# GpSimd makes the low parts of three operands, and the token mixing's last product uses all 128 rows

## The chip, the cores and the metric

The kernel runs on one core of a Trainium2 chip. The metric is the time on the device in microseconds (us). A core has TensorE (PE; its weight loads, PEld, overlap its matmuls), VectorE (DVE), ScalarE (ACT), GpSimd (POOL) and SyncE (SP), which here issues all DMAs. Each engine works through its own instructions in order and waits on semaphores for the others.

## The reference

Three layers follow one another: an attention with mixed heads, a gated layer (the "first layer" after the attention), and a layer with rotated tokens. The change lies in the gated layer, for 4 images ("batch") of 448 tokens:

```python
h = gelu(x @ w_in)                        # 448 x 768 @ 768 x 1024
u, v = h[..., :512], h[..., 512:]
v_n = (v - mu) / np.sqrt(var + 1e-06) * g_ln
v_s = np.einsum('ts,bsd->btd', w_sg, v_n) + b_sg[None, :, None]   # w_sg: 448 x 448
gated = u * v_s
return x + gated @ w_out                  # 512 x 768
```

The weights w_in, w_out and those of the last layer come as 64-bit floats and are decoded on the chip.

## The kernel before, in words

Every float32 matmul operand is split in two: `cast` (line 531, ScalarE) makes the high part, and `rest` (line 534) subtracts it from the value, which leaves the low part. A product is then three matmuls: high by high, high by low, low by high. `mm` (line 538) issues them into one PSUM tile; all matmuls of the dense layers carry that line.

The work of the dense layers is a list of units (`d.unit`), each a group of matmuls with what follows it: `v_chunk` (128 tokens of v), `u_half` (128 features of u), `gate` (the token mixing for 128 features: products with w_sg, then on VectorE `gt` = ps * g_ln + b_sg, times u) and `out` (128 features of the output, with the residual added). For image b the order is: v chunks, half of the out units of image b - 1, four u units, the other out units, four gates. For image 0 it is v, u, gates; for the last image three out units of image 2 stand behind its gates. Hooks before and after a unit (`d.pre`, `d.post`) hold the rest: loads of x, `split_x` (x of the next image, two blocks of 128 rows after each of three units from the end of u on), `split_wsg` (in the first two u units of image 0), normalisation and split of v, `gate_split` (g, one unit after its gate), stores, and the `tick`s of the decoder. All order is written out by hand: each engine's queue follows the program's order.

The decoder takes blocks of 128 x 256 words through ScalarE (two conversions and the high part) and VectorE (lines 574, 576, 581, 589, 595, 598: two shifts and masks, a mask, a product, a subtraction, an addition). In this part of the kernel all VectorE steps of a decoded block run on VectorE; the blocks of w_out are needed by the first `out` unit, those of the last layer's weights only later.

448 tokens are three blocks of 128 and a last one of 64. The last 64 tokens of two neighbouring images share a block: image b even takes rows 0 to 63 (`p.start` 0), b odd rows 64 to 127. In `norm_split` the tile `vnm` of each holds the high part in its own 64 rows and the low part in the other 64, and w_sg's last 64 rows stand twice in `wsg[3]`. So `(m, wh)` on 128 rows gives high by high and low by high at once, and `(m[p], wl[p])` on 64 rows gives high by low.

Buffers that matter here: x (one per block and part, reused for the next image), g (one per block and part), `gt` (two), the staging tiles of the loads (four; w_sg and x of the next image go through them).

Of the kernel before, what the change touches and what calls it, by code (L numbers as in the profile page):

```python
# [6 lines left out]
F32 = mybir.dt.float32  # L7
F32R = mybir.dt.float32r
# [4 lines left out]
ALU = mybir.AluOpType  # L13
# [3 lines left out]
B, H, S, D = 4, 12, 448, 64  # L17
# [457 lines left out]
class Dense:  # L475
# [71 lines left out]
    def decode(self, src, n, dst, tiles=None):  # L547

        nc, box = self.nc, {}

        def block(pool, i):
            if tiles:
                return tiles(i)
            if i == 0:
                box["hl"] = pool.tile([128, 2, 256], F32R, tag="dh", name="dh", bufs=self.out_bufs)
            return box["hl"][:, i, :n]

        def load(pool):  # L560
            raw = pool.tile([128, 256, 2], U32, tag="draw", name="draw", bufs=self.raw_bufs)
            nc.sync.dma_start(out=raw.rearrange("p n w -> p (n w)")[:, :2 * n], in_=src.bitcast(U32))
            box["raw"] = raw

        def words(pool, part=None):
            raw = box["raw"]
            if part != 1:
                for t in ("a", "low", "p"):
                    box[t] = pool.tile([128, 256], F32, tag="d" + t[0], name="d" + t[0], bufs=self.mid_bufs)[:, :n]
                nc.scalar.activation(out=box["p"], in_=raw[:, :n, 1].bitcast(F32), func=AF.Copy, scale=2.0 ** -112)  # L570
                nc.scalar.activation(out=box["low"], in_=raw[:, :n, 0], func=AF.Copy, scale=2.0 ** -52)
            if part != 0:
                au, pu = (box[t].bitcast(U32) for t in "ap")
                nc.vector.tensor_scalar(out=au, in0=pu, scalar1=3, scalar2=0x7FFFFFF8,
                                        op0=ALU.logical_shift_left, op1=ALU.bitwise_and)
                nc.vector.scalar_tensor_tensor(out=au, in0=pu, scalar=0x80000000, in1=au,  # L576
                                               op0=ALU.bitwise_and, op1=ALU.bitwise_or)

        def value(pool):
            a, p = box["a"], box["p"]  # L580
            nc.vector.tensor_scalar(out=p.bitcast(U32), in0=a.bitcast(U32), scalar1=0xFF800000, scalar2=None,
                                    op0=ALU.bitwise_and)

        def high(pool, part=None):
            if part != 1:
                box["h"] = block(pool, 0)
                nc.scalar.activation(out=box["h"], in_=box["a"], func=AF.Copy)
            if part != 0:
                nc.vector.tensor_tensor(out=box["p"], in0=box["p"], in1=box["low"], op=ALU.mult)

        def low(pool, part=None):
            a, p, h = (box[k] for k in ("a", "p", "h"))
            if part != 1:
                box["lo"] = block(pool, 1)
                nc.vector.tensor_tensor(out=a, in0=a, in1=h.bitcast(F32), op=ALU.subtract)
            if part != 0:
                eng = nc.vector if self.mid_bufs > 1 else nc.gpsimd
                eng.tensor_tensor(out=box["lo"], in0=a, in1=p, op=ALU.add)

        def store(pool):  # L600
            if tiles:
                return
            nc.sync.dma_start(out=dst, in_=box["hl"][:, :, :n].bitcast(F32))

        return load, words, value, high, low, store

    def decode_tiles(self, src, rows, c0, c1, tiles):
# [28 lines left out]
def moe1(d, left, right):  # L636

    tc, nc, io = d.tc, d.nc, d.io
    win_es, tail_es, tail_ps = ExitStack(), ExitStack(), ExitStack()
    win, wsg, wout, xt, uT, vraw, mv, vn, mixed, gt, res = ({} for _ in range(11))  # L640
# [62 lines left out]

    def split_wsg(c):
        raw = res.pop(("wsg", c))
        wsg[c] = [d.pools["w"].tile([128, S], F32R, tag=f"wsg{c}{i}", name="wsg") for i in range(2)]
        d.cast(wsg[c][0], raw)
        d.rest(nc.vector, wsg[c][1], raw, wsg[c][0])

    def load_x(b, k):  # L710
        raw = d.stage(512, "xraw")
# [6 lines left out]
    def split_x(b, k):  # L718
        if k == 0:
            xt[b] = ([], [])  # L720
        raw = res.pop(("x", b, k))
        n = 512 if b % 2 == 0 else S
        h, l = (d.pools["x"].tile([128, 512], F32R, tag=f"x{i}{k}", name="x") for i in range(2))
        d.cast(h[:, :n], raw[:, :n])
        d.rest(nc.vector, l[:, :n], raw[:, :n], h[:, :n])
        xt[b][0].append(h)
        xt[b][1].append(l)

# [62 lines left out]
    def gate(b, f):  # L791
        if f == 0:
            gt[b] = ([], [])
        m, p = mixed[b]
        fs = slice(128 * f, 128 * f + 128)
        ps = d.ps()
        terms = []
        for c in range(3):
            (h, l), (wh, wl) = vn[b, c], wsg[c]
            terms += [(h[:, fs], wh), (h[:, fs], wl), (l[:, fs], wh)]  # L800
        wh, wl = wsg[3]
        terms += [(m[:, fs], wh), (m[p, fs], wl[p])]
        d.mm(ps[:, :S], terms)
        t = d.pools["t"].tile([128, S], F32, tag="gt", name="gt")
        nc.vector.scalar_tensor_tensor(out=t, in0=ps[:, :S], scalar=small["gln"][:, f:f + 1], in1=small["bsg"],
                                       op0=ALU.mult, op1=ALU.add)
        nc.vector.tensor_tensor(out=t, in0=t, in1=uT[b][f], op=ALU.mult)
        res["g", b, f] = t

    def gate_split(b, f):  # L810
        t = res.pop(("g", b, f))
        h, l = (d.pools["g"].tile([128, S], F32R, tag=f"g{f}{i}", name="g") for i in range(2))
        d.cast(h, t)
        d.rest(nc.vector, l, t, h)
        gt[b][0].append(h)
        gt[b][1].append(l)

# [22 lines left out]
    for b in range(B + 1):  # L840
        if b < B:
            nv = 4 if b % 2 == 0 else 3
            v0[b] = len(d.units)
            for c in range(nv):
                d.post(U(v_chunk, b, c), v_stats, b, c)
        if b:
            o0[b - 1] = [U(out, b - 1, m) for m in range(KD // 2 if b != B - 1 else NO2)]
        if b < B:
            u0[b] = len(d.units)
            for f in range(KF):  # L850
                U(u_half, b, f)
        if 0 < b < B - 1 or b == B:
            o0[b - 1] += [U(out, b - 1, m) for m in range(KD // 2, KD)]
        if b < B:
            g0[b] = len(d.units)
            for f in range(KF):
                i = U(gate, b, f)
                late.append((d.post, i + 1, gate_split, b, f))
        if b == B - 1:
            o0[b - 1] += [U(out, b - 1, m) for m in range(NO2, KD)]  # L860
# [3 lines left out]
    for c in range(4):  # L864
        d.post(u0[0] + c // 2, split_wsg, c)
    for b in range(B):
        nv = 4 if b % 2 == 0 else 3
        if b:
            d.pre(o0[b - 1][0] + 1, sdev, b)
        for c in range(nv):  # L870
            i = o0[b - 1][0] + 1 + c if b else u0[0] + c // 2
            if b:
                d.post(i, norm, b, c)
            d.post(i, norm_split, b, c)
        if b + 1 < B:
            i = u0[b] + KF
            for k in range(KD):
                d.pre(i - 2 + k // 2, load_x, b + 1, k)
                d.post(i + k // 2, split_x, b + 1, k)
        for m in range(KD):  # L880
            d.pre(o0[b][m] - 1, load_res, b, m)
            d.post(min(o0[b][m] + 1, end - 1), store, b, m)
# [21 lines left out]
    for k in range(KD):  # L904
        at(-7 if k < 4 else -5, load_x, 0, k)
        at(-5 + k // 2, split_x, 0, k)
# [370 lines left out]
```

## Time and profile before

| | |
|---|---|
| median of 3 runs | 932.59 us (931.76 to 936.1) |
| the profiled execution | 931.18 us |
| its span, first to last instruction | 929.4 us |
| PE busy in the span | 886.8 us (95%) |
| PEld busy | 677.9 us (73%) |
| DVE busy | 681.2 us (73%) |
| ACT busy | 525.2 us (57%) |
| POOL busy | 249.0 us (27%) |
| mean granted clock of TensorE | 0.987 |

All times of the rows below are of that one execution, counted from the span's start. Busy time is the union of an engine's instructions; a matmul's end is modelled, so the distance between starts says more than its length. "Idle before" is the time an engine stood still ahead of an instruction, with what released it; "issue" means that nothing the profile shows did.

### The profile page before, as it was taken

The numbers are of one execution on the slowest core, as the hardware profiler recorded it, in microseconds if no ns is written. First come the engines' busy times: TensorE is split into PE (matmuls) and PEld (weight loads), VectorE is DVE, ScalarE is ACT, GpSimd is POOL, SyncE is SP. The second block draws the span as 40 slices with busy tenths as digits, with TensorE's granted clock in tenths as the row PEclk, the third lists the DMA queues.
The fourth block names the chain that finished last, engine by engine and source line by source line (L and its number), as shares of the span: only waits on it lengthen the run. The fifth ranks groups of instructions, "written<-read, shape, count | busy, mean of one in ns | idle before, by whom it ended". The sixth has DMA issues, their size and how long they took to land.

```text
span 929.4 us, 28674 instructions
## 1 busy us (share of the span) xinstructions
PE 886.8 (95%) x11632; PEld 677.9 (73%) x11632; DVE 681.2 (73%) x1512; ACT 525.2 (57%) x1188; POOL 249.0 (27%) x450
## 2 busy tenths in 40 slices
PE   7899999999999999799899999989998999999998
PEld 2455555555555555577697988879898999999997
DVE  2787888788778887569988989768879339638421
ACT  4688788878898886457564564534634125214210
POOL 0272236224522442000000000014615506703511
PEclk9999999999999999899999999999999999999999
DMA  4657756775677555764368575897630302120211
GB/s 157 202 180 219 211 168 202 224 212 176 201 225 212 177 180 134 250 221 142 99 210 254 185 236 178 259 328 230 221 107 25 109 28 52 60 60 18 90 30 60
DMA packets 126963, 151.80 MB, mean 163 GB/s; under 512 B 26352, under 2 KB 112624, under 8 KB 126832
## 3 DMA queue, kind: packets, MB, share of 16 engines
q1 hardware_dynamic: 126832, 149.97, 51.7%
q8 instruction: 92, 1.51, 0.7%
q14 instruction: 39, 0.32, 0.1%
HBM read 79.09 MB, written 32.31 MB: 120 GB/s over the span
## 4 chain that ended last, share of the span: by engine, by line
PE 66%; DVE 15%; DMA 6%; ACT 6%; issue 3%; POOL 2%; SPq 1%; ACTq 0%; DVEq 0%; POOLq 0%
PE ps L538 44%; PE psC L282 6%; PE psA L200 5%; PE psB L224 5%; PE psD L334 4%; ACT e L238 3%; DVE al L311 2%; DMA blk<-s 2%; DVE nmx L230 1%; ACT s L206 1%; DMA vraw<-in_vN 1%; DMA win<-win_d 1%; ACT ah L305 1%; DVE da L576 1%; PE ps L1032 1%
## 5 line engine op out<-in xcount | busy, mean ns | idle before, releaser
L238 ACT ACTIVATE e<-psB,nmx 128x448 f32<-128x448 f32 x180 | 112.6, 630 | 58.2 <-DVE nmx L230 57.3
L311 DVE SCALAR_TENSOR_TENSOR al<-psC,ah 128x480 f16<-128x480 f32 x180 | 109.3, 648 | 8.2 <-ACT ah L305 7.2
L230 DVE TENSOR_REDUCE nmx<-psB 128x1 f32<-128x448 f32 x180 | 103.4, 615 | 13.1 <-PE psB L224 12.7
L534 POOL TENSOR_TENSOR x2s<-x,x2s 128x384 fp32r<-128x384 f32 x28 | 29.9, 1089 | 307.6 <-ACT x2s L531 307.6
L224 PE MATMUL psB<-blk,kpre 64*64 64x448 f32 x720 | 103.6, 565 | 5.5 <-DMA blk<-s 2.6
L282 PE MATMUL psC<-wr,e 64*64 64x60 f32 x5632 | 104.2, 222 | 1.1 <-POOL wr L260 0.7
L538 PE MATMUL ps<-wtok,z 128*128 128x448 f32 x504 | 104.8, 368 | 0.0
L200 PE MATMUL psA<-k,q 64*120 64x448 f32 (+1 forms) x384 | 96.8, 579 | 7.3 <-ACT s L206 5.8
L538 PEld LDWEIGHTS ps<-wtok,z 128*128 128x128 f32 x504 | 94.6, 188 | 9.5
L282 PEld LDWEIGHTS psC<-wr,e 64*64 64x64 f32 x5632 | 92.2, 135 | 12.6 <-POOL wr L260 5.7
L334 PEld LDWEIGHTS <-vh 128*64 128x64 f16 x1536 | 57.0, 111 | 56.9 <-issue 56.7
L538 PE MATMUL ps<-wth,x2s 128*128 128x384 f32 x504 | 95.1, 345 | 3.4 <-POOL x2s L534 1.9
L305 ACT ACTIVATE ah<-psC 128x480 f16<-128x480 f32 x180 | 92.9, 573 | 3.9 <-PE psC L282 3.4
L538 PEld LDWEIGHTS ps<-wth,x2s 128*128 128x128 f32 x504 | 90.1, 194 | 4.1 <-POOL x2s L534 2.2
L206 ACT ACTIVATE s<-psA 120x896 f32<-120x896 f32 (+1 forms) x90 | 83.2, 924 | 16.5 <-PE psA L200 10.0
L538 PE MATMUL ps<-u,wch 128*128 128x448 f32 x432 | 89.9, 368 | 0.0
L538 PEld LDWEIGHTS ps<-u,wch 128*128 128x128 f32 x432 | 81.1, 188 | 8.1
L534 POOL TENSOR_TENSOR z<-zz,z 128x384 fp32r<-128x384 f32 x56 | 61.9, 1126 | 73.4 <-ACT z L531 73.3
L244 POOL TENSOR_SCALAR rc<-sum 128x2 f32<-128x2 f32 (+1 forms) x92 | 20.3, 221 | 209.0 <-ACT e L238 208.7
L224 PEld LDWEIGHTS psB<-blk,kpre 64*64 64x64 f32 x720 | 24.7, 131 | 70.0 <-ACT e L238 46.9
L538 PE MATMUL ps<-g,wout 128*128 128x448 f32 x288 | 63.3, 378 | 5.7 <-DVE g L534 3.3
L260 POOL TENSOR_SCALAR wr<-w,rc 128x60 f32<-128x60 f32 x180 | 54.5, 317 | 44.2 <-DVE rc L249 34.5
(126 smaller groups left out, 1585.5 us busy)
## 6 DMA issues: line engine op xcount, KB each, us to landing
blk<-s SPq DMA_DIRECT2D x176, 210.0 KB
vraw<-in_vN SPq DMA_DIRECT2D x24, 256.0 KB
draw<-in_w_in SPq DMA_DIRECT2D x24, 256.0 KB
k<-in_kvT SPq DMA_DIRECT2D x24, 224.0 KB
xraw<-xT SPq DMA_DIRECT2D x24, 224.0 KB
xres<-xT SPq DMA_DIRECT2D x24, 224.0 KB
x2T<-xres SPq DMA_DIRECT2D x24, 224.0 KB
xres<-x2T SPq DMA_DIRECT2D x24, 224.0 KB
```

Source lines behind the costliest of these rows:

```text
L200: nc.tensor.matmul(ps[e][:n, :S], q[p, o:o + n], k[p], start=True, stop=True)
L206: nc.scalar.activation(out=out, in_=pair[:n, :, :S], func=AF.Copy, scale=0.125)
L224: nc.tensor.matmul(ps[e][c:c + 64, :S], kpre[k, e], blk[k], start=True, stop=True)
L230: nc.vector.tensor_reduce(out=nmx[r][:, e:e + 1], in_=ps[:, :S], axis=AX.X, op=ALU.max, negate=True)
L238: nc.scalar.activation(out=x, in_=ps[:, :S], func=AF.Exp, bias=m[:, e:e + 1], accum_out=sm[:, e:e + 1])
L260: nc.gpsimd.tensor_scalar(out=w, in0=wts[n], scalar1=rc[:, e:e + 1], scalar2=0.0, op0=ALU.mult, op1=ALU.add)
L282: nc.tensor.matmul(pc[r][h][c:c + 64, jc, :, SQ * e:SQ * e + SQ], x[p, c:c + 64], wr[r][e][p], start=(e == 0 and jc == 0), stop=(e == 1 an ...
L305: nc.scalar.activation(out=at_view(r, e, at[b, t][0]), in_=at_src(r, e), func=AF.Copy, scale=2.0 ** -17)
L311: nc.vector.scalar_tensor_tensor(out=al, in0=at_src(r, e), scalar=2.0 ** -17, in1=ah, op0=ALU.mult, op1=ALU.subtract)
L334: nc.tensor.matmul(ps[p, o:o + n], v[:, jc, p], a[:, i0:i0 + n], start=(o == 0 and m == 0), stop=(o > TI and m == len(terms) - 1))
L534: eng.tensor_tensor(out=out, in0=in_, in1=hi.bitcast(F32), op=ALU.subtract)
L538: self.nc.tensor.matmul(ps, l, r, start=(i == 0), stop=(i == len(terms) - 1))
```

## The change

`rest` is given GpSimd for w_sg, for g, and for x of images 1 to 3 (x of image 0 stays on VectorE). The low part of w_sg's last block becomes two tiles, one for each position of the 64 rows, with zeros in the other half, which GpSimd clears; the gate's last matmul then runs on all 128 rows with the tile of its image. In the decoder the mask behind the first shift is left out.

```diff
@@ decode, words @@
-                nc.vector.tensor_scalar(out=au, in0=pu, scalar1=3, scalar2=0x7FFFFFF8,
-                                        op0=ALU.logical_shift_left, op1=ALU.bitwise_and)
+                nc.vector.tensor_scalar(out=au, in0=pu, scalar1=3, scalar2=None, op0=ALU.logical_shift_left)
@@ split_wsg @@
-        wsg[c] = [d.pools["w"].tile([128, S], F32R, tag=f"wsg{c}{i}", name="wsg") for i in range(2)]
+        wsg[c] = [d.pools["w"].tile([128, S], F32R, tag=f"wsg{c}{i}", name="wsg") for i in range(2 if c < 3 else 3)]
         d.cast(wsg[c][0], raw)
-        d.rest(nc.vector, wsg[c][1], raw, wsg[c][0])
+        if c < 3:
+            d.rest(nc.gpsimd, wsg[c][1], raw, wsg[c][0])
+            return
+        for e in range(2):
+            p, o = slice(64 * e, 64 * e + 64), slice(64 - 64 * e, 128 - 64 * e)
+            nc.gpsimd.memset(wsg[c][1 + e][o].bitcast(F32), 0.0)
+            d.rest(nc.gpsimd, wsg[c][1 + e][p], raw[p], wsg[c][0][p])
@@ split_x @@
-        d.rest(nc.vector, l[:, :n], raw[:, :n], h[:, :n])
+        d.rest(nc.gpsimd if b else nc.vector, l[:, :n], raw[:, :n], h[:, :n])
@@ gate @@
-        wh, wl = wsg[3]
-        terms += [(m[:, fs], wh), (m[p, fs], wl[p])]
+        terms += [(m[:, fs], wsg[3][0]), (m[:, fs], wsg[3][1 + p.start // 64])]
@@ gate_split @@
-        d.rest(nc.vector, l, t, h)
+        d.rest(nc.gpsimd, l, t, h)
```

## Rows read from the trace of the kernel before

**Rows 1.** Chain of waits, 415 to 615 us: start, length, what.

```profile
421.43 1.07 DVE wsg L534 x2
...
459.15 146.89 PE ps L538 x678
```

**Rows 2.** Busy time by stretches: length, then PE, PEld, DVE, ACT, POOL.

```profile
430.00:440.00 10.00, 10.00 (x43) 7.46 (x42) 9.68 (x29) 5.62 (x13) 0.00 (x0) 1.00 0.52 167
...
490.00:500.00 10.00, 10.00 (x42) 7.53 (x43) 8.22 (x21) 5.53 (x13) 0.00 (x0) 1.00 0.93 286
...
550.00:560.00 10.00, 10.00 (x44) 7.81 (x43) 8.97 (x22) 3.69 (x9) 0.00 (x0) 1.00 0.86 264
```

**Rows 3.** Waits of PE, 419 to 625 us: total, times, longest.

```profile
PE ps L538 <- DVE g L534: 3.3, 3, 2.1
PE ps L538 <- DVE x L534: 3.1, 2, 1.7
PE ps L538 <- DVE wout L598: 2.4, 1, 2.4
```

**Rows 4.** DVE by line and shape, 460 to 612 us: busy us, mean ns.

```profile
L574 DVE TENSOR_SCALAR da<-dp 128x256 uint32<-128x256 uint32 x35 | 10.0, 286 | 0.7 <-ACT dp L570 0.7
L581 DVE TENSOR_SCALAR dp<-da 128x256 uint32<-128x256 uint32 x35 | 10.0, 285 | 0.0
```

**Rows 5.** Timeline of PEld inside image 1's gates: start, length, idle before.

```profile
492.55 0.18 PEld L538 LDWEIGHTS ps<-wsg,vnm 64*128 64x128 f32 x1 [0.31 <-issue]
492.94 0.30 PEld L538 LDWEIGHTS ps<-wsg,vn 128*128 128x128 f32 x2 [0.21 <-ACT dh L587]
```

**Rows 6.** Timeline of PE, 489 to 537 us.

```profile
490.32 2.09 PE L538 MATMUL ps<-wsg,vn 128*128 128x448 f32 x9
...
492.95 2.09 PE L538 MATMUL ps<-wsg,vn 128*128 128x448 f32 x9
...
521.98 14.76 PE L538 MATMUL ps<-x,win 128*128 128x448 f32 x72
536.57 0.77 PE L538 MATMUL ps<-g,wout 128*128 128x448 f32 x3
```

**Rows 7.** DVE by line and shape, 419.3 to 459.2 us.

```profile
L805 DVE SCALAR_TENSOR_TENSOR gt<-ps,gln,bsg 128x448 f32<-128x448 f32 x4 | 2.7, 679 | 0.1
```

**Rows 8.** Instructions of line 1111 (last layer): duration min/median/max in ns.

```profile
L1111 POOL TENSOR_TENSOR uu<-u x24: 1145/1150/1162, 723.8 to 913.5; 128x448 f32<-128x448 f32 x24
```

**Rows 9.** Timeline, 672.5 to 677.1 us: DVE beside POOL.

```profile
674.03 2.10 POOL L534 TENSOR_TENSOR x2s<-x,x2s 128x384 fp32r<-128x384 f32 x2
674.04 1.23 DVE L962 TENSOR_SCALAR ch<-ch 128x384 uint32<-128x384 uint32 x1 [1.86 <-ACT ch L960]
675.30 1.25 DVE L964 SCALAR_TENSOR_TENSOR ch<-ch,ch 128x384 uint32<-128x384 uint32 x1
676.65 0.36 DVE L966 TENSOR_SCALAR ch<-ch 128x384 uint32<-128x384 uint32 x1
677.05 0.56 DVE L967 TENSOR_TENSOR ch<-ch,wchraw 128x384 f32<-128x384 f32 x1
```

**Rows 10.** DVE by line and shape, 640 to 680 us.

```profile
L1047 DVE SCALAR_TENSOR_TENSOR r<-n,r 128x384 f32<-128x384 f32 x8 | 7.5, 936 | 0.3
L1048 DVE TENSOR_SCALAR r<-r 128x384 f32<-128x384 f32 x8 | 7.0, 878 | 0.3
L1046 DVE SCALAR_TENSOR_TENSOR r<-n,ps 128x384 f32<-128x384 f32 x7 | 3.9, 554 | 0.2
```

**Rows 11.** POOL by line, 640 to 680 us.

```profile
L534 POOL TENSOR_TENSOR z<-zz,z 128x384 fp32r<-128x384 f32 x16 | 17.9, 1141 | 13.1 <-ACT z L531 13.1
L534 POOL TENSOR_TENSOR x2s<-x,x2s 128x384 fp32r<-128x384 f32 x8 | 8.4, 1070 | 0.0
```

**Rows 12.** Timeline, 513.8 to 517.2 us, as out of image 1 begins.

```profile
514.69 2.79 PE L538 MATMUL ps<-g,wout 128*128 128x448 f32 x13
...
515.24 0.59 DVE L534 TENSOR_TENSOR g<-gt,g 128x448 fp32r<-128x448 f32 x1
```

## The prediction

> **What bounds the kernel now.** I read the chain of waits first, because VectorE (73% busy) and TensorE (95%) both look like bounds over the whole span. In the first layer the chain changes hands once: from about 420 to 459 us it runs through VectorE almost alone (the low parts of w_sg among it), and from 459.15 on it is one piece of TensorE, 147 us long [rows 1]. The busy time by stretches shows the same: VectorE is busy 9.68 of 10 us at 430:440, where TensorE ends the stretch waiting; inside the TensorE piece VectorE still works 8.2 to 9.0 of 10 us [rows 2], so it has little to spare there either. The waits of TensorE say what it lacked: 3.1 us for low parts of x, 2.4 us for a decoded block of w_out, 3.3 us for low parts of g [rows 3]. All three are VectorE's output. GpSimd does nothing in any of these stretches [rows 2]. So two sums are needed: what VectorE gains or loses up to 459 us, and what of TensorE's saving survives after it.
>
> **The decoder's operation.** I went to the groups of VectorE by shape next. The shift with its mask takes 286 ns, the neighbour with one operation on the same shape 285 ns [rows 4]. An operation more inside one instruction costs nothing that shows; no instruction disappears. I take 0; the bounds are one ns either way for each of the 80 blocks, 0.1 us.
>
> **The last product on all 128 rows.** Each gate is 11 matmuls, the last on 64 rows. In front of its weight load TensorE's loader stands 0.31 us with no releaser but "issue", and 0.21 us in front of the next one [rows 5]. From one gate to the next it is 492.95 - 490.32 = 2.63 us; 72 equal matmuls without such a switch take 536.57 - 521.98 = 14.59 us, 0.2026 each [rows 6], so 11 would take 2.23. The change gives back 0.40 us a gate, 1.6 us for each of four images, 6.4 in all. Bounds: 0 if the pause belongs to the end of the group rather than to the 64 rows, and 0.52 if both pauses go whole. The product streams the same 448 columns; I take rows of zeros at the price of rows of data.
>
> **The subtractions that move.** 38 of them: w_sg 4 (which become 5, as the last is made in two halves), x 18, g 16. On VectorE two of them fill 1.07 us of the chain, 0.535 each [rows 1]. On GpSimd the same shape with both operands in SBUF takes 1.15 us [rows 8]. GpSimd's time itself is free here; two things are not.
>
> First, the price on VectorE. At 674 us two such GpSimd instructions (384 columns, 2.10 us together) run beside two VectorE instructions that read and write only SBUF: these take 1.23 and 1.25 us, where the same kinds with GpSimd quiet take 0.36 and 0.56 [rows 9]. That is 0.87 + 0.69 = 1.56 us lost for two, 0.78 each; scaled by 1.15/1.05 to 448 columns, 0.85. Instructions that read one operand from PSUM aren't stretched: 554 ns beside the same GpSimd work, against 936 for the kind with both in SBUF [rows 10]. VectorE's queue up to 459 us is nearly all of the stretched kind: the six decoder instructions of a block, the normalisation, the product with u; the gate's first operation (0.68 us, four times) reads PSUM and gives cover [rows 7]. Bounds of the price: below, the mean over 640:680, where 8 x (0.936 - 0.56) + 8 x (0.878 - 0.36) + 1.56 = 8.7 us are lost beside 16 + 8 GpSimd subtractions [rows 10, 11], 0.36 each, 0.40 scaled; above, the whole 1.15 us. I take 0.85, since VectorE here has as little PSUM work as at 674 us.
>
> The Trainium skill (SBUF — State Buffer, Who interferes with whom) says that the two engines share a port pair under an exclusive lock, and that the second one to issue is blocked until the first finishes; by it a subtraction costs the whole 1.15 us. The trace shows 74% of that, 0.78 of 1.05. By the rule the sum below would be 11.3 us slower instead of 2.1.
>
> Second, latency. GpSimd works in order: x0, x1, x2, x3, g0, x4, x5, g1, g2, g3 after the first gates. Behind a late one stand the next v product (x), the out products (g), VectorE's gate operation (its buffer gt has two copies, freed by the subtraction) and, on SP's queue, the loads of x into staging buffers that the w_sg subtraction frees. Up to 459 us all of it lies behind VectorE's own lateness, so I cost it at nothing; if that cover goes it is 0.6 us (1.15 - 0.535) for the last of each series.
>
> **The sum**, with p the price of one subtraction.
> - To 459 us: 15 subtractions x 0.85 x 0.9 (a tenth hidden by PSUM reads: 4 x 0.68 of 39.8 us, and the batch statistics) = 11.5; VectorE sheds 14 x 0.535 = 7.5; the two clearings of half tiles have no row, at least 0, at most as long as the shortest stretched loss, 0.69 each; I take 0.1 each, as they only write. +4.2 us. The first image's 1.6 us on TensorE is lost, because it waits for VectorE anyway.
> - Images 1 and 2 (TensorE's piece): the first has 6 subtractions of 512 columns and 4 of 448: 6 x 0.97 + 4 x 0.85 = 9.2, times 0.83 (residual adds and gate operations read PSUM) = 7.7, less 5.8 shed: VectorE +1.9. It idles 1.8 us at 490:500 [rows 2], so about 0. But the last low part of g is done at 515.83 [rows 12], and the out product that began at 514.69 reads it in its twelfth matmul, 11 x 0.2026 later, at 516.9: TensorE can come forward by 1.1 of its 1.6 us. -1.1. The second: 7.1 less 5.35 = +1.7, idle 1.0 at 550:560 [rows 2], the same 1.1 taken as slack: -0.4.
> - Image 3: TensorE -1.6; the final low parts of g, for which it waits already [rows 3], come later by 0.5 to 1.4 us (one longer subtraction, or that and one stretched decoder block); I take 0.9. -0.7.
>
> 4.2 - 1.1 - 0.4 - 0.7 = **+2.0 us**. The profiled execution took 931.18 us (span 929.4 and 1.8 around it), 1.4 under the median of the runs, 932.59. So 933.2 in a profile, **934.6** as a median. Half a per cent, 4.7 us, is what a measurement of this kernel can tell from no change.
>
> **Rivals.**
> - *Slower: VectorE is blocked longer than 0.85 us each.* All of VectorE's decoder work before 459 us is of the stretched kind, and a waiting GpSimd instruction can in turn cost VectorE its overlap between neighbours. With p: 13.5p - 7.3 to 459 us; 9.0p - 8.7 and 8.3p - 7.45 in the two images (neither under -1.6); -0.7. It passes +4.7 us at p = 0.94; at p = 1.15 it is +11.3, 943.9 us. Against it: the 74% of rows 9. Chance 0.33.
> - *Faster: the subtractions fall beside PSUM reads and VectorE's idle time, as on average in 640:680.* At p = 0.40: -1.9 - 1.6 - 1.6 - 0.7 = -5.8, 926.8 us. It passes -4.7 at about p = 0.48. For it: that mean, and that a delayed VectorE leaves GpSimd waiting for its casts, so that they spread out. Against it: the casts of x and w_sg come in pairs into decoder work. Chance 0.25.
> - *The last product saves nothing, since the pause belongs to the group's end.* Against it: the pause stands on both sides of the 64-row load, inside the group too. Then +4.2, nothing in images 1 and 2 (VectorE's 0.1 and 0.7 stay under the slack of 1.1), and 0.9: +5.1, 937.7 us. Chance 0.05.
> - The forecast itself, p from 0.48 to 0.94: 0.37.
>
> Faster by over 0.5%: 0.25. Within: 0.37. Slower: 0.33 + 0.05 = 0.38. The range takes in p = 0.35 to 1.1: 926 to 943 us. The forecast's own range is 928 to 937.
>
> **What would show it.** Right: the 64-row load is gone, gates 2.2 us apart; L595, L598, L576 and L581 beside a GpSimd subtraction 0.7 us or more above their 0.42 or 0.28, L805 unchanged; TensorE's wait for w_out of 2.4 us grown to some 6; TensorE's long piece starting near 463 us. Wrong: decoder instructions at their old length beside GpSimd (then faster), a long piece that starts before 459, or waits for x or g of several us at the head of the v and out products (then latency, not price, decides).

## The result, and the profile after

The changed kernel takes **939.88 us** (median of 10 runs, 935.99 to 947.17), the kernel before 933.71 in the same comparison (10 runs): a ratio of 1.0075, with a 95% interval of 1.0053 to 1.0097. That is slower by over 0.5%, to which the prediction gave a chance of 0.38. The wide range of 926 to 943 us holds it; the forecast itself, 934.6 us with 928 to 937 as its own range, did not come. The profiled execution took 938.18 us, its span 936.4 against 929.4: 7.0 us, where the prediction had 2.0.

The page's busy times (span share, instructions) show little of it: VectorE shed 38 subtractions and is busy 8.6 us longer, GpSimd 50.6 us longer.

```profile
PE 885.7 (95%) x11632; PEld 681.5 (73%) x11632; DVE 689.8 (74%) x1474; ACT 524.6 (56%) x1188; POOL 299.6 (32%) x491
```

Where the 7 us are is read from the starts of TensorE's pieces. First two marks of the kernel before that were not shown yet (timeline of PE): its first gate, and the end of the changed part, the first theta product of the last layer.

```profile
428.04 1.99 PE L538 MATMUL ps<-wsg,vn 128*128 128x448 f32 x9
...
626.49 3.29 PE L538 MATMUL ps<-wth,x2s 128*128 128x384 f32 x18
```

The same view of the changed kernel (start, length, last in brackets the idle time and its releaser):

```profile
427.65 1.78 PE L538 MATMUL ps<-wsg,vn 128*128 128x448 f32 x8
430.87 0.47 PE L538 MATMUL ps<-wsg,vn 128*128 128x448 f32 x1 [1.44 <-DVE vn L534]
...
457.93 2.19 PE L538 MATMUL ps<-g,wout 128*128 128x448 f32 x10
465.02 7.08 PE L538 MATMUL ps<-g,wout 128*128 128x448 f32 x26 [4.90 <-DVE wout L597]
...
496.08 2.02 PE L538 MATMUL ps<-wsg,vn 128*128 128x448 f32 x9
...
498.36 2.02 PE L538 MATMUL ps<-wsg,vn 128*128 128x448 f32 x9
...
519.64 2.47 PE L538 MATMUL ps<-g,wout 128*128 128x448 f32 x11
522.91 5.33 PE L538 MATMUL ps<-g,wout 128*128 128x448 f32 x25 [0.79 <-POOL g L534]
528.08 15.03 PE L538 MATMUL ps<-x,win 128*128 128x448 f32 x72
...
571.58 1.98 PE L538 MATMUL ps<-g,wout 128*128 128x448 f32 x9
575.45 0.68 PE L538 MATMUL ps<-g,wout 128*128 128x448 f32 x2 [1.89 <-ACT g L531]
576.91 6.90 PE L538 MATMUL ps<-g,wout 128*128 128x448 f32 x25 [0.79 <-POOL g L534]
583.65 14.76 PE L538 MATMUL ps<-x,win 128*128 128x448 f32 x72
...
633.54 3.29 PE L538 MATMUL ps<-wth,x2s 128*128 128x384 f32 x18
```

Two stretches are used from here on. **(a)** runs from the first gate to the eleventh matmul of the first out unit, the one that needs the decoded block of w_out: 31.1 us before (428.04 to 459.15), 37.4 after. **(b)** runs from there to the first theta product: 167.3 before, 168.5 after. The first gate comes 0.4 us earlier, and the last layer takes 302.9 us in both: -0.4 + 6.3 + 1.2 = 7.1, the whole difference but for rounding. So nearly all of the loss lies where VectorE set the end already, and of the 4.2 us that the gates of images 1 to 3 give back on TensorE (12 x 0.35) nothing is left.

The gates did become shorter: 498.36 - 496.08 = 2.28 us apart, 2.63 before [rows 6], and the loader goes from gate to gate without the two pauses of [rows 5] (timeline of PEld inside image 1's gates):

```profile
500.01 0.39 PEld L538 LDWEIGHTS ps<-wsg,vnm 128*128 128x128 f32 x2
500.43 1.84 PEld L538 LDWEIGHTS ps<-wsg,vn 128*128 128x128 f32 x9
```

TensorE's waits, 419 to 635 us (total, times, longest), beside [rows 3]: that for w_out grew from 2.4 to 4.9 us, and those for g changed hands, from VectorE to ScalarE and GpSimd.

```profile
PE ps L538 <- DVE wout L597: 4.9, 1, 4.9
PE ps L538 <- POOL g L534: 3.0, 4, 0.9
PE ps L538 <- ACT g L531: 2.6, 2, 1.9
PE ps L538 <- ACT x L531: 2.1, 1, 2.1
```

What VectorE lost up to 465 us stands in its instructions by shape (busy us, mean ns), 419.1 to 465 us, after. Before, the same kinds took 425, 417, 425, 285, 416, 285 and 540 ns; the gate's first operation, which reads PSUM, took 679 [rows 7].

```profile
L597 DVE TENSOR_TENSOR wout<-da,dp 128x256 fp32r<-128x256 f32 x10 | 6.8, 679 | 0.3
L588 DVE TENSOR_TENSOR dp<-dp,dl 128x256 f32<-128x256 f32 x11 | 6.5, 594 | 0.0
L575 DVE SCALAR_TENSOR_TENSOR da<-dp,da 128x256 uint32<-128x256 uint32 x10 | 6.0, 598 | 0.3
L580 DVE TENSOR_SCALAR dp<-da 128x256 uint32<-128x256 uint32 x10 | 5.7, 572 | 0.0
L594 DVE TENSOR_TENSOR da<-da,wout 128x256 f32<-128x256 f32 x10 | 5.1, 510 | 0.0
L574 DVE TENSOR_SCALAR da<-dp 128x256 uint32<-128x256 uint32 x10 | 5.1, 509 | 0.0
L763 DVE TENSOR_SCALAR v<-v,mv,sd 128x512 f32<-128x512 f32 x4 | 3.6, 961 | 0.0
L809 DVE SCALAR_TENSOR_TENSOR gt<-ps,gln,bsg 128x448 f32<-128x448 f32 x4 | 2.7, 677 | 0.0
```

Beside these 15 GpSimd subtractions VectorE lost, as count times added mean, 2.5 + 1.9 + 1.7 + 2.9 + 0.9 + 2.2 + 1.7 = 14.0 us (in the order of the lines, unrounded sum). VectorE shed 7.5 us here (14 subtractions of 0.535), so it should end 6.5 us later; (a) grew by 6.3. Over the 15 subtractions it is 0.93 us each. The timeline shows single cases: a VectorE instruction that begins under a GpSimd subtraction takes some 1.25 us, whatever it takes alone (0.28 to 0.42), and ends a little behind the subtraction: 439.28 after the first pair's 438.99, 441.93 after the second pair's 441.65. L580, which begins before the second pair, keeps its 0.28. L809 begins behind the pairs, so its 0.67 says nothing on PSUM reads.

```profile
436.54 2.45 POOL L534 TENSOR_TENSOR x<-xraw,x 128x448 fp32r<-128x448 f32 x2 [7.82 <-issue]
436.71 1.27 DVE L597 TENSOR_TENSOR wout<-da,dp 128x256 fp32r<-128x256 f32 x1
...
437.90 1.38 DVE L588 TENSOR_TENSOR dp<-dp,dl 128x256 f32<-128x256 f32 x1
...
439.21 0.28 DVE L580 TENSOR_SCALAR dp<-da 128x256 uint32<-128x256 uint32 x1
439.32 2.33 POOL L534 TENSOR_TENSOR x<-xraw,x 128x448 fp32r<-128x448 f32 x2 [0.32 <-ACT x L531]
439.41 1.24 DVE L574 TENSOR_SCALAR da<-dp 128x256 uint32<-128x256 uint32 x1
...
440.68 1.25 DVE L575 SCALAR_TENSOR_TENSOR da<-dp,da 128x256 uint32<-128x256 uint32 x1
...
441.86 0.67 DVE L809 SCALAR_TENSOR_TENSOR gt<-ps,gln,bsg 128x448 f32<-128x448 f32 x1
```

No L809 up to 465 us begins while GpSimd subtracts. What speaks on PSUM reads is the residual add L837, which reads one operand there: seven of them begin under subtractions between 495 and 619 us and take 0.61 to 0.62 us, the mean of the kernel before being 0.614.

### The profile page after: what moved, and what is told of

It reads as the page before. It is cut to its first block, busy times and chain, and to the rows that moved or that the text cites. A ratio compares the mean times of both kernels' runs of the same rounds, so it can differ in the third digit from the quotient of the medians.

```text
span 936.4 us, 28725 instructions
## 1 busy us (share of the span) xinstructions
PE 885.7 (95%) x11632; PEld 681.5 (73%) x11632; DVE 689.8 (74%) x1474; ACT 524.6 (56%) x1188; POOL 299.6 (32%) x491
## 4 chain that ended last, share of the span: by engine, by line
PE 42%; DVE 28%; DMA 11%; ACT 8%; issue 6%; POOL 3%; SPq 1%; ACTq 0%; DVEq 0%; POOLq 0%
PE ps L538 24%; PE psC L282 5%; PE psA L200 4%; PE psB L224 4%; ACT e L238 4%; PE psD L334 3%; DVE al L311 3%; DMA xres<-xT 3%; DVE da L594 3%; DVE dp L588 2%; DVE dh L597 2%; DMA blk<-s 2%; DVE nmx L230 2%; DVE dp L580 2%; DMA win<-win_d 2%
## 5 line engine op out<-in xcount | busy, mean ns | idle before, releaser
L230 DVE TENSOR_REDUCE nmx<-psB 128x1 f32<-128x448 f32 x180 | 103.5, 616 | 11.3 <-PE psB L224 10.9
L538 PE MATMUL ps<-g,wout 128*128 128x448 f32 x288 | 65.8, 386 | 10.5 <-DVE wout L597 4.9
L538 PE MATMUL ps<-win,x 128*128 128x512 f32 x252 | 66.1, 420 | 6.2 <-DMA win<-win_d 2.8
L538 PEld LDWEIGHTS ps<-g,wout 128*128 128x128 f32 x288 | 57.2, 201 | 18.3 <-DVE wout L597 5.3
```

Of the source, the lines that this page charges most:

```text
L230: nc.vector.tensor_reduce(out=nmx[r][:, e:e + 1], in_=ps[:, :S], axis=AX.X, op=ALU.max, negate=True)
L538: self.nc.tensor.matmul(ps, l, r, start=(i == 0), stop=(i == len(terms) - 1))
```

## The experiments

The theory: GpSimd's subtractions stretch VectorE's SBUF-only instructions, by more than VectorE sheds. The rivals: GpSimd delivers its low parts too late, with VectorE's speed untouched (latency); or the gates save less than their spacing says. Kernels of one group below ran on one chip and share the runs of the kernel before. The time ahead of the first gate varies from one execution to the next (426.97 and 432.15 us in two profiles of the same kernel), so the stretches (a) and (b) are compared beside the medians; they come from one profiled execution of each kernel.

| run | median us | ratio to before, 95% | (a) us | (b) us |
|---|---|---|---|---|
| before | | | 31.1 | 167.3 |
| after | 939.88 | 1.0075 (1.0053 to 1.0097) | 37.4 | 168.5 |
| e1_gate_rows | 929.17 | 0.9928 (0.991 to 0.9945) | 31.8 | 164.4 |
| e2_moves_alone | 940.95 | 1.0068 (1.0044 to 1.0093) | 36.2 | 168.2 |
| e3_later_only | 934.78 | 1.0005 (0.998 to 1.0029) | 31.8 | 167.9 |
| e4_shadow | 956.97 | 1.0234 (1.0208 to 1.026) | 40.1 | 179.5 |
| e5_x_alone | 933.75 | 1.0011 (0.9984 to 1.0037) | 34.0 | 166.4 |
| e6_g_alone | 934.39 | 1.0022 (0.9996 to 1.0049) | 32.6 | 168.1 |
| e7_wsg_alone | 931.77 | 0.9988 (0.9963 to 1.0013) | 33.7 | 165.0 |
| e8_columns | 930.43 | 0.9979 (0.9953 to 1.0005) | 29.3 | 169.2 |
| e9_gate_again | 931.61 | 0.9976 (0.9955 to 0.9998) | 31.8 | 165.7 |
| e10_relief | 926.92 | 0.9931 (0.9904 to 0.9957) | 27.3 | 161.9 |
| e11_after_relief | 937.15 | 1.0025 (0.9998 to 1.0052) | 32.7 | 167.0 |
| e12_after_again | 941.16 | 1.0094 (1.0062 to 1.0127) | 37.4 | 167.9 |

The kernel before had medians of 935.25 (e1 to e4), 932.87 (e5 to e8) and 934.75 (e9 to e12).

**The gate alone.** To the kernel before, only the last product on 128 rows is added; all low parts stay on VectorE, GpSimd only clears the halves.

```diff
+        for e in range(2):
+            p, o = slice(64 * e, 64 * e + 64), slice(64 - 64 * e, 128 - 64 * e)
+            nc.gpsimd.memset(wsg[c][1 + e][o].bitcast(F32), 0.0)
+            d.rest(nc.vector, wsg[c][1 + e][p], raw[p], wsg[c][0][p])
...
-        terms += [(m[:, fs], wh), (m[p, fs], wl[p])]
+        terms += [(m[:, fs], wsg[3][0]), (m[:, fs], wsg[3][1 + p.start // 64])]
```

> Only the last product of the token mixing on all 128 rows (two half-cleared low tiles, cleared by GpSimd); every low part is made by VectorE. Price theory (GpSimd's subtractions block VectorE's SBUF-only instructions): no subtraction runs on GpSimd, VectorE has one subtraction more before 459 us (+0.5), gates 2.28 us apart instead of 2.63; TensorE's long piece starts at about 459.7 and keeps 1.1 us in images 1 and 2 and 1.4 in image 3: 2.5 to 3.5 us faster than before. Rival (the saving is always eaten by VectorE's lateness at out): 0 to 0.5 us slower. Rival (the pause belongs to the group's end): gates stay 2.63 us apart.

Faster by 0.72%; a second measurement on another chip (e9, below) gives 0.24%, where 0.3 to 0.8 was expected. (a) + (b) of the two profiled executions falls by 2.3 and 0.9 us, less than expected. The medians fell by more, 6.1 and 3.1 us; where the rest was won isn't shown. The mechanism holds: gates stand 2.27 us apart (timeline of PE).

```profile
488.29 2.02 PE L538 MATMUL ps<-wsg,vn 128*128 128x448 f32 x9
...
490.56 2.02 PE L538 MATMUL ps<-wsg,vn 128*128 128x448 f32 x9
```

But TensorE then waits more for VectorE (its waits, 419 to 640 us): 6.4 us for x, against 3.1 before.

```profile
PE ps L538 <- DVE x L534: 6.4, 4, 2.7
```

**The moves alone.** The three `rest` calls go to GpSimd, the gate stays on 64 rows.

```diff
-        d.rest(nc.vector, wsg[c][1], raw, wsg[c][0])
+        d.rest(nc.gpsimd, wsg[c][1], raw, wsg[c][0])
...
-        d.rest(nc.vector, l[:, :n], raw[:, :n], h[:, :n])
+        d.rest(nc.gpsimd if b else nc.vector, l[:, :n], raw[:, :n], h[:, :n])
...
-        d.rest(nc.vector, l, t, h)
+        d.rest(nc.gpsimd, l, t, h)
```

> Only the three moves of subtractions to GpSimd, the last product on 64 rows as before, the decoder as before. Price theory: 14 subtractions lose 0.9 us each before 459 us and save 7.5, so the long piece starts 5 us late; images 1 to 3 add what the changed kernel lost there (1.1 us net) and the 4.2 us that its gates gave back: 9 to 11 us slower than before. Latency theory (only the longer way through GpSimd counts, at the heads of v and out): 2 to 4 us slower, the long piece starts within 1 us of 459.

0.68% slower, 6.4 us; (a) + (b) grew by 6.0. That is the whole loss of the change, without the gate's rows. The expected 9 to 11 us are missed because they add the gate's saving back: with the moves in place that saving is worth almost nothing, (b) being 168.2 without it and 168.5 or 167.9 with it.

**GpSimd only after the first stretch.** The changed kernel, but w_sg, x of image 1 and g of image 0 stay on VectorE.

```diff
-            d.rest(nc.gpsimd, wsg[c][1 + e][p], raw[p], wsg[c][0][p])
+            d.rest(nc.vector, wsg[c][1 + e][p], raw[p], wsg[c][0][p])
...
-        d.rest(nc.gpsimd if b else nc.vector, l[:, :n], raw[:, :n], h[:, :n])
+        d.rest(nc.gpsimd if b > 1 else nc.vector, l[:, :n], raw[:, :n], h[:, :n])
...
-        d.rest(nc.gpsimd, l, t, h)
+        d.rest(nc.gpsimd if b else nc.vector, l, t, h)
```

> The changed kernel, but w_sg, x of image 1 and g of image 0 stay on VectorE, so GpSimd subtracts nothing before 459 us (two clearings remain); x of images 2 and 3 and g of images 1 to 3 stay on GpSimd. Price theory: the long piece starts within 1 us of 459.7, the 5.9 us of the first stretch are gone, and what is left is the 1.1 us the changed kernel loses after it: 0 to 2 us slower than before. Rival (VectorE's lateness from the first stretch is what makes the later stalls): 3 us faster than before, no waits of TensorE for g at out.

The time is that of before, and (a) is back to 31.8 us, that of e1. So the first stretch's loss comes from the subtractions in it. But (b) is 167.9, 3.5 and 2.2 us over e1 and e9: the moves cost something in images 1 to 3 too, of their own and not as lateness carried over.

**A shadow.** VectorE keeps everything; GpSimd subtracts each high part of the same tiles from itself into a tile that nobody reads. No product waits for these instructions, and VectorE sheds nothing.

```diff
+    def shadow(self, hi):
+        t = self.pools["w"].tile([128, S], F32, tag="sh", name="sh")
+        hi = hi[:, :S].bitcast(F32)
+        self.nc.gpsimd.tensor_tensor(out=t, in0=hi, in1=hi, op=ALU.subtract)
```

> The kernel before, with every low part still made by VectorE; behind each of the 38 subtractions of w_sg, x of images 1 to 3 and g, GpSimd subtracts the high part from itself into a scratch tile that nobody reads (448 columns). The output is the reference's; the extra work is idle work. Price theory: VectorE sheds nothing and loses 0.9 us for each of 14 before 459 us, so the long piece starts 12 us late; images 1 and 2 add 3 to 6 us each: 18 to 25 us slower. Latency theory: nobody waits for these instructions, so the time is that of before within 1 us.

2.34% slower, 21.9 us, from work that no engine waits for in the trace. The latency rival, which expected nothing, falls as the cause of the first stretch's loss. (a) grew by 9.0 us. VectorE's lines show it, here with its own subtraction of g among the stretched (by shape, 423 to 472 us), and GpSimd's below them:

```profile
L594 DVE TENSOR_TENSOR dp<-dp,dl 128x256 f32<-128x256 f32 x11 | 6.8, 617 | 0.0
L603 DVE TENSOR_TENSOR wout<-da,dp 128x256 fp32r<-128x256 f32 x10 | 6.2, 620 | 0.3
...
L534 DVE TENSOR_TENSOR g<-gt,g 128x448 fp32r<-128x448 f32 x4 | 3.9, 980 | 0.0
```

```profile
L539 POOL TENSOR_TENSOR sh<-x 128x448 f32<-128x448 f32 x6 | 5.8, 975 | 11.1 <-ACT x L531 10.8
L539 POOL TENSOR_TENSOR sh<-wsg 128x448 f32<-128x448 f32 x4 | 4.3, 1063 | 40.9 <-ACT wsg L531 40.7
```

A subtraction of a tile from itself takes 0.98 to 1.06 us, not 1.23 to 1.35 as with two tiles, and 9.0 / 14 = 0.64 us are lost for each. The expected size in (a) supposed the longer instruction.

**Each move on top of the gate's rows.** e1 with one `rest` call each on GpSimd: x, g, or w_sg.

> The last product on 128 rows as in e1, and of the three moves only that of x (images 1 to 3) to GpSimd. Price theory: 6 subtractions before 459 us lose 0.9 each and save 3.2, so the long piece starts about 2.2 us later than in e1; images 1 and 2 lose about 1 us each at out: 3 to 5 us slower than e1. Latency theory: the waits of TensorE for x at the head of the v product grow by up to 1 us for each of three images, nothing at w_out.

> As e1, and of the three moves only that of g (16) to GpSimd. Price theory: 4 before 459 us lose 0.9 each and save 2.1: the long piece starts 1.5 us later than in e1; 4 in each later image, 0.5 to 1 us each at out, and up to 1 us at the last four: 2.5 to 5 us slower than e1. Latency theory: 0.6 us more waiting for g at the head of each out series, 2 us in all, w_out unchanged.

> As e1, and of the three moves only that of w_sg (4 tiles, 5 subtractions, all before 428 us) to GpSimd. Price theory: 5 x 0.9 - 5 x 0.535: the long piece starts 1.8 us later than in e1 and the whole is 1 to 2 us slower. Latency theory: nothing waits for w_sg first, so 0, or 2 us faster for what VectorE sheds.

In (a) they add 2.2, 0.8 and 1.9 us to e1's, where 2.2, 1.5 and 1.8 were expected; x and w_sg as worked out, g less. In (a) + (b) they add 4.2, 4.5 and 2.5 us (2.9, 3.2 and 1.1 over e9), together 11.2 (7.2), beside 9.7 (8.4) for all three in one kernel. No move gains. These runs are on another chip than e1 and e9, so it is the stretches that carry the comparison. Where g costs is plain from two pieces, TensorE's first out units of images 1 and 2 (from their first matmul to the next u product, 36 matmuls):

| | before | e1 | e5 x | e6 g | e7 w_sg | after | e3 | e4 shadow |
|---|---|---|---|---|---|---|---|---|
| image 1's, us | 7.29 | 7.29 | 7.29 | 8.40 | 7.28 | 8.44 | 8.14 | 8.71 |
| image 2's, us | 7.29 | 8.30 | 8.80 | 11.81 | 8.31 | 12.07 | 12.71 | 11.87 |

Of the three moves only that of g loses clearly there, 1.1 and 3.5 us over e1. But e4 loses as much, and there g's low part stays on VectorE: it is enough that GpSimd works beside VectorE at g's time.

**w_out by columns.** e1, with one operation in the decoder's first shift as in the change, and the blocks of w_out decoded column by column, so that what the first out unit needs comes first.

```diff
+        by_k = []
...
-            d.jobs += d.decode_tiles(io["w_out"], slice(128 * k, 128 * k + 128), 0, DM, tiles)
+            by_k.append(d.decode_tiles(io["w_out"], slice(128 * k, 128 * k + 128), 0, DM, tiles))
+        d.jobs += [job for column in zip(*by_k) for job in column]
```

> As e1, with the one-operation shift of the decoder, and w_out's blocks decoded by columns (first block of all four row groups, then the second, then the third) instead of by rows. If VectorE's lateness is what ends the stretch before 459 us, the first out unit now needs the fourth decoded block instead of the tenth, 12 us of decoder work less: TensorE's wait for w_out (2.4 us) goes, the waits for x stay: 2 to 4 us faster than e1. If the stretch is bound by the wait for x instead, the time is that of e1 within 1 us.

The wait for w_out is gone, (a) is 2.5 us shorter than e1's, and the median says nothing came of it: (b) is 4.9 us longer. TensorE now reaches the v product behind image 1's gates before x is ready for it, and after these waits (2.0 us for ScalarE's part of x and 1.6 for VectorE's, 484 to 520 us) its granted clock is low (busy times by stretch; the share behind POOL's is the clock):

```profile
500.00:510.00 10.00, 9.81 (x31) 7.85 (x32) 9.65 (x23) 4.95 (x13) 0.00 (x0) 0.69 0.65 224
```

The expectation (2 to 4 us faster than e1) missed because it took a wait removed early for time won. VectorE was still as late as before, so TensorE waited further on. The shift with one operation takes 287 ns here, 286 with two [rows 4].

**Less decoder work where VectorE is late.** e10 is e8 with decoder ticks moved from the v units of image 1 and a gate of image 0 to the out units of image 3; e11 is the changed kernel with both, e9 and e12 are e1 and the changed kernel again.

```diff
-TV = ((), (2, 2, 2), (1, 1, 1, 1), (1, 1, 1))
+TV = ((), (1, 1, 1), (1, 1, 1, 1), (1, 1, 1))
...
-TG = ((1, 0, 1, 1), (1, 0, 1, 0), (1, 0, 1, 0), (1, 1, 0, 0))
-TO = ((1, 1, 1, 1, 1, 1), (1, 0, 1, 0, 1, 0), (1, 0, 1, 0, 1, 1), (0, 1, 1, 1, 1, 0))
+TG = ((0, 0, 1, 1), (1, 0, 1, 0), (1, 0, 1, 0), (1, 1, 0, 0))
+TO = ((1, 1, 1, 1, 1, 1), (1, 0, 1, 0, 1, 0), (1, 0, 1, 0, 1, 1), (1, 1, 2, 2, 1, 1))
```

> The kernel of e1 once more, on the chip and beside the runs of the next three. Price theory: 3 us of its trace from the long piece's start to the last layer, and up to 0.7% by the clock of single runs: 0.3 to 0.8% faster than before.

> The kernel of e8, with four of the decoder's blocks taken out of the units between 433 and 515 us and put beside the last image's out units, where VectorE idles. If VectorE's sum of work up to the out units of image 1 is the bound, 8 us of it are gone there: the waits for x at 440 us and at the v product of image 1 go, the stretch to the first out unit is 2 to 4 us shorter than in e9 and out of image 1 starts 5 us or more earlier: 3 to 6 us faster than e9. Rival (latency of single operations): as e8.

> The changed kernel with the same two edits of the decoder's order (columns of w_out; four blocks put off). GpSimd's subtractions stay. If the changed kernel is slower only since VectorE's queue is full while GpSimd blocks it, 8 us less work there takes most of it back: 5 to 8 us faster than the changed kernel, no wait for w_out, waits for g under 2 us in all. Latency theory: the waits for x and g behind GpSimd stay as they are, and it is 0 to 3 us faster than the changed kernel (the wait for w_out alone).

> The changed kernel once more, on the same chip: 0.5 to 1.0% slower than before, its trace with 13 to 15 us of VectorE stretched in the 15 subtractions before the first out unit.

e10 is the fastest of its chip: 926.92 us, 0.9931 of before, 4.7 us under e9, inside the 3 to 6 expected. (e1 had 0.9928 on its own chip.) TensorE goes through the first out units without a wait for w_out (timeline of PE: 36 matmuls in one piece), and its remaining waits for g and x are 3.3 and 2.9 us.

```profile
460.49 7.45 PE L538 MATMUL ps<-g,wout 128*128 128x448 f32 x36
```

(a) + (b) is 9.3 us shorter than before, of which some 3 come back in the last layer (306.0 us from the first theta product to the end, against 302.9); that this is the postponed decoder work isn't shown, for e11, which postpones the same work, takes 303.7 there, and the other kernels 301.8 to 304.4. What the four moved blocks win without the column order was not run.

e11 is 4.0 us under e12, between the two expectations (5 to 8, and 0 to 3 by latency). Its (a) is 4.7 us shorter, without the wait for w_out. It is still 10.2 us over e10: the same order of work with GpSimd's part in it. Its waits for g stay at 5.3 us, where under 2 were expected; image 2's out piece takes 13.89 us (e10: 7.64). e12 repeats the changed kernel: 0.94% slower, 37.4 us in (a), 14.0 us of VectorE lost beside the 15 subtractions as expected (13 to 15), 12.08 us in image 2's out piece.

## Why the prediction was right or wrong

**The decoder's operation**: right, it saves nothing (287 ns in e8, 286 before). **The gate**: right in kind, 0.35 us each (2.63 to 2.28) instead of 0.40. The pauses of [rows 5] are gone.

**The term that failed by its size: the price of one subtraction up to 459 us.** The prediction took 0.85 us and a tenth of cover, 0.765. Measured were 0.93, or 0.91 without the 0.36 us lost beside a clearing (below): nothing was hidden by PSUM reads, since none of the four gate operations begins under a subtraction here. 11.5 became 14.0 us, +4.2 became 6.3. In the slower rival's own term for this stretch, 13.5p, 13.6 to 14.0 us are p = 1.01 to 1.04: past the 0.94 from which that rival passes 4.7 us, short of its 1.15. In the images the 0.71 below is p = 0.78. The Trainium skill (SBUF — State Buffer, Who interferes with whom) says that whichever of the two engines issues first holds the shared ports for its whole instruction, and that the other is blocked. The trace agrees: under each of the 15 subtractions one VectorE instruction begins 0.02 to 0.43 us behind its start and ends 0.15 to 0.29 us behind its end (timeline, 419 to 465 us). VectorE loses 0.91 of a subtraction's 1.15 us [rows 8], 79%, because that instruction begins later than the subtraction, and its own 0.28 to 0.54 us would have passed anyway. So the sum at the whole 1.15, +11.3, is 4.3 us above the measured 7.0, and the forecast is 5.0 below it.

**The step that failed in its reasoning: images 1 and 2.** TensorE was to keep 1.1 and 0.4 us of its gates' saving. By TensorE's marks (the start of the first out units and of the next u product), it won 0.9 and 1.2 us on the way there and lost 1.15 and 4.78 in those units: +0.2 and +3.6 instead of -1.1 and -0.4. Image 3 gave back 2.7 (0.7 was forecast): 1.4 by its gates, and some 1.2 because the waits for g near 610 us fell from 3.3 to 2.1 us. Together +1.2 us where -2.2 was forecast. Three things were wrong with the step:
- *VectorE's idle time took in less than was counted on.* The forecast set 1.9 and 1.7 us of added VectorE work against 1.8 and 1.0 us of idle time in [rows 2]. From the start of (b) to image 2's last product with u, VectorE works 100.4 us instead of 95.9 (4.4 more) and idles 8.7 instead of 10.5 (1.9 less). So this product starts 2.6 us later, counted from the start of (b); image 1's last one 0.9. About a third of the idle time in (b) before is waits inside VectorE's own chain, and these weren't filled: for ScalarE's cast of vn it waits 6.3 us in nine waits, before and after alike.

```profile
DVE vn L534 <- ACT vn L531: 6.3, 9, 0.7
```

The price in the images was forecast well: between 460 and 620 us VectorE's decoder instructions and products with u lost 17.0 us (means above those of before, times count) beside GpSimd's 24 subtractions, 0.71 each, with 0.77 forecast; here the residual adds give cover.
- *The waits at the head of an out product are this lateness, and only a little latency.* TensorE waits 0.79 us for the last low part of g at 522.91 and again at 576.91; the 1.89 us ahead of the latter are for ScalarE's cast of g, which is late because VectorE's product is. The product and the last low part of image 2, before and after (timelines):

```profile
565.64 0.62 DVE L807 TENSOR_TENSOR gt<-gt,u 128x448 f32<-128x448 f32 x1
...
567.53 0.59 DVE L534 TENSOR_TENSOR g<-gt,g 128x448 fp32r<-128x448 f32 x1
```

```profile
574.10 0.62 DVE L811 TENSOR_TENSOR gt<-gt,u 128x448 f32<-128x448 f32 x1
...
575.47 1.39 POOL L534 TENSOR_TENSOR g<-gt,g 128x448 fp32r<-128x448 f32 x1 [3.39 <-ACT g L531]
```

From the product's start to the end of the low part it is 568.12 - 565.64 = 2.48 us before and 576.86 - 574.10 = 2.76 after. The way through GpSimd costs 0.28 us more, in image 1 too, where 0.6 was held ready. It is so little because before, VectorE put a batch statistic between product and subtraction. The rest is VectorE's 0.9 and 2.6 us, and the 0.9 us by which TensorE itself comes earlier. In e6, which moves g alone, these products start 1.1 and 2.6 us later than in e1.
- *A wait costs more than itself.* After 575 us TensorE, having waited 1.89 and 0.79 us, runs the next 25 matmuls in 583.65 - 576.91 = 6.74 us, where 25 x 0.2026 = 5.07 is the pace of [rows 6]: 1.7 us more. The granted clock shows it: 0.89 and 0.94 over two stretches of 10 us, 1.00 in both before. That is (0.11 + 0.06) x 10 / 0.5 = 3.4 us at 1.2 instead of 2.4 GHz. In e2, whose waits there are 0.69 and 0.80 us, the same 25 matmuls take 5.16 us.

```profile
570.00:580.00 10.00, 7.32 (x29) 5.89 (x28) 9.72 (x22) 5.16 (x14) 3.47 (x3) 0.89 0.43 124
580.00:590.00 10.00, 10.00 (x48) 9.19 (x48) 8.45 (x24) 4.46 (x10) 0.00 (x0) 0.94 0.66 219
```

**The signs named beforehand.** Right: the spacing of the gates and the stretched decoder lines. The unchanged L805 (L809 after) came too, but up to 465 us it never ran beside a subtraction, so it proves nothing there. The wait for w_out came to 4.9 rather than 6 us, the long piece started at 465 rather than 463, since TensorE arrived later too (it had waited for vn and x). Of the signs for wrong, waits of several us for g at the head of an out product did come, in image 2. But latency has only 0.28 us in each of them, and e4 has such waits (0.82 us in image 1, 1.76 and 0.81 in image 2) with g's low part on VectorE: the price decides there too.

**The rivals.** The slower one's mechanism was the one that came, and up to 459 us at more than its threshold. With the images as forecast the sum would still have been 6.3 - 2.2 = 4.1 us; it was the images' term that carried the time over half a per cent. The faster one (p up to 0.48) is excluded by p = 1.01 in the first stretch. That the product saves nothing is excluded by the gates' spacing and e1.

## What to carry to other kernels

An idle GpSimd isn't free help for a VectorE that works from SBUF alone: a subtraction whose move saved VectorE 0.535 us cost it 0.71 to 0.93. By these numbers such a move could pay only where VectorE mostly reads PSUM; no run here shows a case that pays. Before a saving is credited, look at which engine waits behind it: the gate's 5.6 us on TensorE (16 x 0.35) left 0.9 to 2.3 in (a) and (b) by themselves and next to nothing beside the moves, while a better order of the decoder's work, with less of it where VectorE is late, won 4.7 us more. Idle time that is a wait inside an engine's own chain wasn't room for more work here.

## What the runs showed of the hardware

- An operation that only writes can stretch VectorE as well, but not each of its instructions: beside one clearing of 64 rows on GpSimd a shift of 0.29 us took 0.64 (timeline of the changed kernel), while a subtraction of two tiles (L594) that begins under the other clearing, at 427.28, takes 0.41 as ever. It is the same in e7, e11 and e12: 0.64 and 0.41.

```profile
425.35 0.50 POOL L712 MEMSET wsg<- 64x448 f32 x1
425.36 0.64 DVE L574 TENSOR_SCALAR da<-dp 128x256 uint32<-128x256 uint32 x1
```

- The stretching goes both ways: GpSimd's own subtraction, 1.15 us with VectorE quiet or reading PSUM [rows 8], has means of 1.23 to 1.35 beside the decoder (changed kernel, 419 to 465 us, by shape). Single ones take 1.31 to 1.52 when they begin while a VectorE instruction has 0.30 to 0.51 us to go, and 1.15 to 1.19 when it has less than 0.2.

```profile
L534 POOL TENSOR_TENSOR x<-xraw,x 128x448 fp32r<-128x448 f32 x6 | 7.2, 1226 | 8.1 <-issue 7.8 <-ACT x L531 0.3
L534 POOL TENSOR_TENSOR g<-gt,g 128x448 fp32r<-128x448 f32 x4 | 5.4, 1350 | 8.3 <-ACT g L531 8.3
```

- A stretched decoder instruction takes 1.21 to 1.41 us up to 465 us, almost whatever its own length (0.28 to 0.42), since it ends 0.15 to 0.29 us behind the subtraction. So the shortest lose most: the mask of 285 ns lost as much in all (2.9 us) as any kind.
